# A linear-attention and max-out kernel on one core: another order of all its operations and loads

## The chip, the cores and the metric

The kernel runs on one core of a Trainium2 chip. The metric is device time in microseconds (us), taken as the median of several executions. An execution with the hardware profiler on gives a trace; its times are the span from the first instruction to the last on that core. The engines are TensorE (PE, its weight loads PEld), VectorE (DVE), ScalarE (ACT), GpSimd (POOL) and SyncE (SP), which here issues every DMA.

## The reference, cut to what matters

The first half is a recurrent attention with a decay per channel, the second a feed-forward layer whose activation is the larger of two projections. Batch 4, 8 heads, 768 tokens, head size 48; model width 384, inner width 1024.

```python
for t in range(S):
    cur = einsum('bhd,bhe->bhde', u[None] * k[:, :, t], v[:, :, t])
    y[:, :, t] = einsum('bhd,bhde->bhe', r[:, :, t], state + cur)
    state = w[:, :, t][..., None] * state + einsum('bhd,bhe->bhde', k[:, :, t], v[:, :, t])
x = y.transpose(0, 2, 1, 3).reshape(B * S, H * D)
out = maximum(x @ w1, x @ w2) @ w_out
```

## The kernel before

**Tiling.** The tokens are cut into chunks of 256, two neighbouring tokens on each of 128 partitions. There are 8 units of work: units 0 to 3 are the first chunk of batch 0, 1, 2 and 3; units 4 and 5 are the second chunk of two batches each; units 6 and 7 are the third. A chunk needs the state that the chunk before it leaves.

**A unit's steps, in the names that the order uses** (a number behind a name is the unit, further ones are a batch or a part, and @d, @a, @p mean DVE, ACT, POOL). `load` brings w, k, r, v. `wp`, `ln` and, for later units, `hi` and `lo` make logarithms of the decays; `ex` (L395 and L396, for early units L398) sums them along the tokens on PE; `mz`, `e0` (L436) and `ie` (L460) turn the sums into scale factors; `row` (L472), `wl` and `we` carry the chunk's whole decay to another layout through two small DMAs. `rk`, `ru`, `dg`, `dd`, `di` make the diagonal of the score matrix. `rw`, `kw` and `scale` give scaled r and k; `tr` and `te` transpose them on PE and copy them out (units 0 to 4), `dt` (L582) transposes by DMA (units 5 to 7). `sc` (L641) makes the scores, `mk` (L650) copies them under a mask into M, `ya` (L688) multiplies by v, `yi` (L675) adds what the old state gives, `kv` (L596) makes the new state's addend, `st`, `sm`, `sb` update the state. `vb` casts v. `xe` copies the result out of PSUM.

**The second half.** max(a, b) is relu(a − b) + b, so `wdiff` makes w1 − w2, and w2 · w_out is made once: `w2turn` and `w2take` transpose w2, `woload.0` to `woload.3` (L290) load w_out in four quarters, `wocast` casts each quarter to bf16, `wfold` (L318) multiplies, `wctake` copies out. The first matmul of every `wfold` reads the quarter of `woload.0`. Then `gt` (L706) and `rl` (L717, L719) make the relu part, `op` (L725 and L729) adds the two products, `oe` copies out and `os` (L743) stores. `hot` (L234) are 48 matmuls whose results nobody reads; they stand where PE would wait early on.

**What sets the order.** One table, ORDER, lists all 652 steps. They are recorded in this sequence, and each engine gets its instructions in it and runs them strictly one after the other. SP issues the DMAs in the table's order as well. It holds at most eight of them in flight: DMA number n waits for the landing of number n − 8, since eight semaphores take turns. Buffers are few (two tiles each for w, k, r and v, four PSUM banks for `gt`, `op`, `ex`, `wfold`, `tr` and `w2turn` together), so that a step may also wait for a buffer's last reader. The names with a number below, such as lv_174, are tiles: lw, lk, lr, lv hold loads, wso the quarters of w_out, wo_sb the cast w_out, G and Y are PSUM.

Of the kernel before, what the change touches and what calls it, by code (L numbers as in the profile page):

```python
# [59 lines left out]
rw.1.0@d wt.1.0 wload.1.2 ln.2.0 ex.2.0 vb.0.0@a we.0.1 scale.0.0.0.0@d zero.k.0@d kv.0  # L60
scale.0.0.0.1@d tr.0.0.1 dd.0@p mz.2.0 woload.0 we.1.0 ru.1.0@p kw.1.0@p row.2 w2turn.0.0 e0.1.0
scale.1.0.0.0@d st.0.0@a tr.0.0.0 te.0.0.1@a sc.0.0.1.1 sc.0.0.0.1 w2turn.0.1 dg.1 te.0.0.0@a
w2take.0.0@a wload.0.2 load.2.v scale.1.1.0.0@d dd.1@p sb.0.0@a wp.3.0@p tr.1.0.1 e0.2.0 st.0.1
te.1.0.1@a rk.2.0@d zero.M.2@p di.0.0@d ie.2.0 zero.M.0@p rw.2.0@d hot.8.1 wload.1.1 ru.2.0@d
kw.2.0@p scale.2.1.0.0@p sc.0.0.1.0 sc.0.0.0.0 mk.0.0.1.0 vb.1.0@a hot.8.4 mk.0.0.0.0 mk.0.0.1.1
mk.0.0.0.1 vb.1.1@a kv.1 scale.2.0.0.0@d tr.1.0.0 ln.3.0 te.1.0.0@a w2turn.2.1 wdiff.2@p sb.0.1@a
st.1.0@a sb.1.0@a di.1.0@d st.1.1 tr.2.0.0 w2take.0.1@a tr.2.0.1 te.2.0.1@a zero.v.0@d sc.1.0.1.0
w2turn.1.0 wload.0.0 wdiff.0@p w2take.1.0@a sc.1.0.0.0 mk.1.0.1.0 mk.1.0.0.0 sb.1.1@a w2take.2.1@d
w2turn.2.0 w2turn.1.1 w2take.2.0@a hi.3@a ya.0.0.1.0 vb.2.1@a ya.1.0.0.0 sm.0@p sm.1@p wload.0.1
wdiff.1@d ya.1.0.1.0 ya.0.0.0.1 load.3.r trih@a yi.1.0 yi.0.0 ya.0.0.0.0 woload.1 ya.0.0.1.1  # L70
xe.1.0@a xe.0.0@d load.3.k te.2.0.0@a gt.1.3 rl.1.3@a dg.2 rk.3.0@d lo.3@d dd.2@a gt.0.2 rl.0.2@a
wocast.1@p gt.1.1 w2take.1.1@d woload.3 gt.0.0 rw.3.0@p woload.2 rl.0.0@a gt.1.2 load.4.w.0 rl.1.2@a
vb.2.0@p ru.3.0@p gt.0.3 rl.0.3@a ex.3.0 wocast.3@d wocast.2@a wocast.0@a rl.1.1@a di.2.0@d
sc.2.0.1.0 mk.2.0.1.0 gt.0.1 mz.3.0 e0.3.0 kw.3.0@p gt.1.0 dg.3 sc.2.0.0.0 kv.2 st.2.0@a rl.0.1@a
wp.4.0@d ie.3.0 scale.3.0.0.0@d mk.2.0.0.0 wfold.2 sb.2.1@d wfold.0 dd.3@p ln.4.0 load.3.v st.2.1
wfold.1 sb.2.0@d vb.3.0@a wl.2 hi.4@a lo.4@d ya.2.0.0.0 load.4.r rl.1.0@a di.3.0@d vb.3.1@a row.3
ya.2.0.1.0 wctake.1@a we.2 load.4.k wctake.2@a rk.4.0@d wctake.0@a scale.3.1.0.0@p tr.3.0.0 ex.4.0
mz.4.0 tr.3.0.1 ex.4.1 mz.4.1 te.3.0.0@a kv.3 te.3.0.1@a st.3.0@a yi.2.0 xe.2.0@d ie.4.0 op.1.1
oe.1.1@a st.3.1 load.4.v e0.4.0 sb.3.0@a ru.4.0@d gt.2.0 load.5.w.0 rl.2.0@a sc.3.0.0.0 sc.3.0.1.0
vb.4.1@a gt.2.2 op.1.0 rk.4.1@p rw.4.0@d kw.4.0@d scale.4.0.0.0@d scale.4.1.1.0@d scale.4.1.0.0@p  # L80
e0.4.1 rl.2.2@a scale.4.0.1.0@d op.0.1 sb.3.1@a row.4 oe.1.0@a tr.4.1.0 te.4.1.0@a tr.4.1.1 vb.4.0@a
op.0.0 sm.2@p wl.3 mk.3.0.0.0 ya.3.0.0.0 mk.3.0.1.0 ya.3.0.1.0 yi.3.0 oe.0.1@d ru.4.1@p wp.5.0@p
we.3 sm.3@p te.4.1.1@a gt.2.1 xe.3.0@a dg.4 ln.5.0 oe.0.0@d tr.4.0.1 te.4.0.1@a gt.3.0 rl.3.0@a
rl.2.1@a hi.5@a dd.4@d load.5.k kv.4 di.4.0@d sc.4.1.1.0 load.5.r load.5.v rk.5.0@d gt.2.3 rl.2.3@a
gt.3.2 tr.4.0.0 di.4.1@d te.4.0.0@a mk.4.1.1.0 gt.3.3 st.4.0 st.4.1 os.1.0 rl.3.3@a gt.3.1 rl.3.1@a
ru.5.0@p sc.4.1.0.0 rk.5.1@p sc.4.0.0.0 load.6.r sb.4.0@a vb.5.1@a op.2.1 load.6.w.0 lo.5@d wl.4
ex.5.0 mk.4.0.0.0 os.0.0 sb.4.1@a mk.4.1.0.0 oe.2.1@a mz.5.0 e0.5.0 rw.5.0@p ex.5.1 sc.4.0.1.0
load.6.k ru.5.1@p mz.5.1 ya.4.0.0.0 scale.5.0.0.0@d op.2.0 rl.3.2@a op.3.0 mk.4.0.1.0 e0.5.1 os.1.1
scale.5.0.1.0@d dt.5.0.0 ya.4.0.1.0 dt.5.0.1 kw.5.0@d row.5 oe.3.0@d os.3.0 wp.6.0@p ie.5.0
ya.4.1.1.0 ya.4.1.0.0 oe.2.0@d yi.4.1 xe.4.1@d dg.5 dd.5@d scale.5.1.0.0@p di.5.0@d yi.4.0 xe.4.0@a  # L90
op.3.1 rk.6.0@d ln.6.0 hi.6@d gt.4.2 rl.4.2@a lo.6@d gt.4.5 scale.5.1.1.0@p rl.4.5@a os.2.1 gt.4.0
vb.5.0@a gt.4.7 rl.4.7@a we.4 sm.4@p gt.4.4 dt.5.1.0 gt.4.6 sc.5.0.1.0 mk.5.0.1.0 kv.5 oe.3.1@a
rl.4.6@a rl.4.0@a rl.4.4@a st.5.0 gt.4.1 rl.4.1@a sc.5.0.0.0 mk.5.0.0.0 gt.4.3 rl.4.3@a dt.5.1.1
rk.6.1@p st.5.1 ex.6.0 ru.6.1@p sb.5.1@a sb.5.0@a load.6.v os.0.1 vb.6.1@a mz.6.0 ex.6.1 op.4.3
load.7.w.0 load.7.k mz.6.1 e0.6.1 ie.6.0 kw.6.0@d e0.6.0 scale.6.1.1.0@p di.5.1@d sc.5.1.0.0
ya.5.0.1.0 rw.6.0@d ya.5.0.0.0 yi.5.0 xe.5.0@a vb.6.0@a scale.6.0.0.0@d op.4.2 wl.5 os.3.1
scale.6.1.0.0@p sc.5.1.1.0 oe.4.2@a op.4.0 oe.4.3@a oe.4.0@a mk.5.1.0.0 wp.7.0@p ya.5.1.0.0
mk.5.1.1.0 dt.6.0.0 ya.5.1.1.0 yi.5.1 kv.6 scale.6.0.1.0@d dt.6.0.1 xe.5.1@d st.6.0 dt.6.1.1 ln.7.0
op.4.1 sb.6.1@a sb.6.0@a oe.4.1@a ru.6.0@d dg.6 load.7.r dd.6@p gt.5.2 rl.5.2@a gt.5.4 di.6.1@d
gt.5.6 rl.5.6@a hi.7@a gt.5.0 dt.6.1.0 rl.5.0@a gt.5.3 di.6.0@d sc.6.1.1.0 rl.5.3@d rl.5.4@a  # L100
sc.6.1.0.0 gt.5.5 rl.5.5@a os.4.1 gt.5.7 rl.5.7@a rk.7.0@p lo.7@d gt.5.1 we.5 mk.6.1.1.0 rl.5.1@a
ex.7.0 op.5.1 op.5.2 oe.5.2@a sc.6.0.0.0 mk.6.1.0.0 ru.7.0@d mz.7.0 sc.6.0.1.0 mk.6.0.1.0 rk.7.1@p
ex.7.1 mk.6.0.0.0 e0.7.0 mz.7.1 op.5.3 oe.5.1@a load.7.v vb.7.1@a sm.5@p rw.7.0@p ie.7.0 os.2.0
ya.6.0.1.0 os.5.2 os.4.0 ya.6.1.0.0 ya.6.0.0.0 oe.5.3@a os.4.3 kw.7.0@p scale.7.1.1.0@p
scale.7.0.0.0@d ya.6.1.1.0 yi.6.0 xe.6.0@a scale.7.1.0.0@d dt.7.0.0 dt.7.1.0 yi.6.1 op.5.0 vb.7.0@p
xe.6.1@a gt.6.5 oe.5.0@d os.5.0 e0.7.1 gt.6.3 rl.6.3@a rl.6.5@a scale.7.0.1.0@d dt.7.1.1 gt.6.2
dt.7.0.1 os.4.2 kv.7 gt.6.6 gt.6.0 rl.6.6@a os.5.1 st.7.0 gt.6.1 rl.6.2@a ru.7.1@p dg.7 sb.7.1@a
# [690 lines left out]
```

## Time and profile before

| | |
|---|---|
| median of 3 runs | 146.53 us (146.47 to 146.93) |
| the profiled execution, span | 147.2 us |
| its instructions | 5536, of them 2403 matmuls |
| first and last matmul | start at 1.79 us, end at 143.8 us |
| DMA | 31.84 MB, mean 216 GB/s |

The profiled execution is 0.7 us longer than the median of the runs. A row of the timeline gives the start, how long the group took, the engine and line, what was written from what, the count, and in square brackets the engine's idle time ahead of it with what ended it. Matmuls overlap in their pipeline, so that a group's time has a tail that the next group runs in: the step from one start to the next is what PE pays. A row of the windows gives, for a stretch of time, each engine's busy time and count, the granted TensorE clock, the share of the DMA engines' time in use and their rate.

### The profile page before, as it was taken

Reading aid. Unit: us, or ns where it says so; the run is one execution under the profiler, and the core shown is the slowest. Engines: PE = TensorE matmul, PEld = TensorE weight load, DVE = VectorE, ACT = ScalarE, POOL = GpSimd, SP = SyncE. Lnnn points to the kernel's source line nnn. Section 1 sums busy time; section 2 is a strip of 40 time slices with the busy share of each in tenths; the row PEclk is TensorE's granted clock in tenths of the full one; section 3 lists DMA queues with packets and bytes.
Section 4 is the critical chain, followed back from the end, with each engine's and each line's share of the span. In section 5 each row is a group of like instructions: output and inputs, shape, how many; then the busy total and the mean of one; then the engine's idle time right before and its main releaser. Section 6 shows DMA issues by size and latency. Waiting matters only on the chain.

```text
span 147.2 us, 5536 instructions
## 1 busy us (share of the span) xinstructions
PE 136.8 (93%) x2403; PEld 84.2 (57%) x2404; DVE 116.9 (79%) x162; ACT 90.6 (62%) x164; POOL 90.0 (61%) x106
## 2 busy tenths in 40 slices
...
GB/s 104 323 325 357 335 401 394 366 286 304 214 241 277 212 226 282 312 255 174 205 192 177 292 251 207 141 138 291 250 136 78 131 271 20 0 210 62 4 56 157
DMA packets 71186, 31.84 MB, mean 216 GB/s; under 512 B 66293, under 2 KB 70390, under 8 KB 71162
## 3 DMA queue, kind: packets, MB, share of 16 engines
...
q8 instruction: 19, 0.31, 0.8%
q14 instruction: 5, 0.04, 0.2%
...
## 4 chain that ended last, share of the span: by engine, by line
PE 41%; DVE 35%; issue 6%; POOL 6%; DMA 4%; ACT 3%; SPq 2%; DVEq 0%; POOLq 0%; ACTq 0%
PE G L729 12%; DVE M L650 9%; PE G L706 8%; PE G L234 7%; PE G L725 5%; DVE rp L176 4%; DMA lv<-in_v_dram 4%; DVE rku L176 3%; DVE dg L502 3%; POOL kp L180 3%; DVE M L516 3%; PE Y L688 2%; SPq L582 2%; POOL rku L180 2%; PE Y L675 2%
## 5 line engine op out<-in xcount | busy, mean ns | idle before, releaser
L729 PE MATMUL G<-wo_sb,gT 128*128 128x384 bf16 x192 | 35.8, 331 | 0.0
L706 PE MATMUL G<-xT,wd_sb 128*128 128x256 bf16 (+1 forms) x192 | 34.4, 326 | 0.7 <-ACT xT L168 0.6
L650 DVE CAST_PREDICATED M<-mask,Y 128x1024 bf16<-128x1024 int32 (+1 forms) x26 | 28.6, 1131 | 2.8 <-PE Y L641 1.9
L717 ACT ACTIVATE gT<-G 128x512 bf16<-128x512 f32 x43 | 24.5, 601 | 9.8 <-PE G L706 9.6
L729 PEld LDWEIGHTS <-gT 128*128 128x128 bf16 x192 | 19.0, 99 | 12.6 <-issue 0.3
L706 PEld LDWEIGHTS <-wd_sb 128*128 128x128 bf16 x192 | 17.9, 98 | 12.6 <-DVE wd_sb L176 0.6
L180 POOL TENSOR_TENSOR kp<-lk,iE 128x384 bf16<-128x384 f32 x16 | 17.1, 1096 | 9.3 <-DVE lk L176 4.2
L725 PE MATMUL G<-wc_sb,xT 128*128 128x384 bf16 x72 | 15.7, 327 | 0.0
L180 POOL TENSOR_TENSOR rku<-rku,u_b 128x384 f32<-128x384 f32 x14 | 14.5, 1053 | 2.0 <-DVE rku L176 2.0
L234 PE MATMUL G<-S_b 128*128 128x512 bf16 x47 | 13.6, 442 | 1.8 <-DVE S_b L263 1.8
L168 ACT COPY RK<-G 128x1024 bf16<-128x1024 bf16 x12 | 12.1, 1019 | 4.7 <-PE G L565 4.7
L168 ACT COPY osb<-G 128x384 f32<-128x384 f32 x7 | 3.4, 479 | 15.9 <-PE G L729 12.6
L180 POOL TENSOR_TENSOR rku<-lr,lk 128x384 f32<-128x384 f32 x8 | 10.9, 1393 | 2.5 <-DMA lk<-in_k_dram 1.7
L641 PE MATMUL Y<-RK 48*64 48x128 bf16 x384 | 9.0, 220 | 2.6 <-DVE M L650 2.4
L502 DVE TENSOR_REDUCE dg<-rku 128x16 f32<-128x768 f32 x12 | 11.0, 945 | 0.1
L641 PEld LDWEIGHTS <-RK 48*64 48x64 bf16 x384 | 6.2, 106 | 7.8 <-issue 6.7
L168 ACT CAST xT<-Y 128x768 bf16<-128x768 f32 x7 | 7.0, 1025 | 5.3 <-PE Y L675 4.0
L168 ACT CAST S_b<-S_f 64x768 bf16<-64x768 f32 (+1 forms) x14 | 8.7, 624 | 2.3 <-DVE S_f L612 2.0
L176 DVE TENSOR_TENSOR rp<-lr,G 128x768 bf16<-128x768 f32 (+2 forms) x11 | 8.8, 799 | 1.4 <-ACT G L436 1.4
L234 PEld LDWEIGHTS <-S_b 128*128 128x128 bf16 x48 | 5.1, 112 | 8.3 <-issue 3.3
L516 DVE TENSOR_TENSOR M<-identq,gd 128x512 int32<-128x512 int32 x12 | 9.2, 778 | 0.4 <-POOL gd L168 0.3
L168 DVE CAST xT<-Y 128x768 bf16<-128x768 f32 x5 | 5.1, 1017 | 5.5 <-PE Y L688 3.2
...
## 6 DMA issues: line engine op xcount, KB each, us to landing
...
```

Of the source, the lines that this page charges most:

```text
L168: (nc.scalar.copy if e == "a" else nc.vector.tensor_copy if e == "d" else nc.gpsimd.tensor_copy)(o, i)
L176: op(o, a, b)
L180: op(o[:, g], a[:, g], b[:, g])
L234: nc.tensor.matmul(t, zz[:, 0:P], zz[:, 0:512], start=True, stop=True)
L502: nc.vector.reduce_sum(s.dg[:, b].rearrange("p i h -> p h i"), s.rku[:, b], axis=AX.X)
L516: (nc.vector if en == "d" else nc.gpsimd).tensor_tensor(out=o, in0=m, in1=g.unsqueeze(3).to_broadcast([P, 2, H, Q // 2]), op=ALU.bitwise_and)
L641: nc.tensor.matmul(t[q * Q:(q + 1) * Q, e, p * P:(p + 1) * P].rearrange("s (i g) -> s i g", i=2), s.kT[d, b, j, y * n + p, q, :], s.rT[d, ...
L650: nc.vector.copy_predicated(t[:, :, 2 * n * y:2 * n * (y + 1)].rearrange("s i (p e) g -> s p e i g", e=2), mask[:, j].bitcast(I32).unsquee ...
L706: nc.tensor.matmul(t[:, m * n * P:(m + 1) * n * P].rearrange("c (b t) -> c b t", t=P), wd_sb[:, ko, fo * P:(fo + 1) * P], s.xT[:, 0:n, ko, :],
L717: nc.scalar.activation(o, i, AF.Relu)
L725: nc.tensor.matmul(t[:, 0:HD], s.xT[:, a, ko, :], wc_sb[:, ko, :], start=(ko == 0), stop=False)
L729: nc.tensor.matmul(t[:, 0:HD], s.gT[:, c:c + P], wo_sb[:, f, :], start=False, stop=(f == FO - 1))
```

## The change

Only the table ORDER is different. It has the same 652 steps and the same 48 filler matmuls; nothing in the code of a step changes. All steps may stand at another place, and 94 of them run on another engine than before. The list was sought with a model that also counts how fast TensorE's instructions can be supplied. Four lines of the diff:

```diff
-ident zero.s.1@p identq@a load.0.k load.0.r zero.m@p identb@p u zero.s.0@d zero.r@d rk.0.0@d
...
+zero.v.0@p zero.k.1@d zero.M.0@p zero.o@p zero.k.0@d zero.s.0@d hot.8.1 hot.8.4 tri zero.M.1@d
...
+wdiff.1@p load.3.v woload.0 load.4.r wp.4.0@p wocast.0@p wfold.1 wctake.1@a dd.2@a load.4.k wfold.2
+kv.2 st.2.0@a sb.2.1@a wctake.2@a rw.3.0@d st.2.1 wl.2 kw.3.0@d ya.1.0.0.0 di.2.0@d ya.1.0.1.0
...
```

Of the 94 steps, the groups with the most work are: `scale` (6 from POOL to DVE, 1 the other way), `oe` (8 from DVE to ACT, 1 the other way), `xe` (5 from DVE to ACT, 3 the other way), `ru` (4 from POOL to DVE, 2 the other way), `wdiff` (2 from POOL to DVE, 1 the other way) and `vb` (3 from POOL to ACT).

**SP, the loads of the weights and of unit 3.** Before, from the last load of w1 on: r of unit 3, the quarter `woload.1` (wso_291, whose other half `woload.0` stands earlier), k of unit 3, the quarters 3 and 2 (wso_762), w of unit 4, v of unit 3.

```order
L285 DMA gT_383<-in_moe_w1_dram 128x1024
L372 DMA lr_220<-in_r_dram 128x8x96
L290 DMA wso_291<-in_moe_w_out_dram 128x2x384
L372 DMA lk_224<-in_k_dram 128x8x96
L290 DMA wso_762<-in_moe_w_out_dram 128x2x384 x2
L372 DMA lw_781<-in_w_dram 128x8x96 x2
L372 DMA lv_346<-in_v_dram 128x8x96
L478 DMA WL_932<-row_297 128x4x1
```

Now, from the quarters 2 and 3 (wso_336) on; the last row but one is `woload.0` (wso_214), and row_659 is `row.3`, which reads what `mz.3` wrote to MZ.

```order
L290 DMA wso_336<-in_moe_w_out_dram 128x2x384 x2
L285 DMA gT_199<-in_moe_w1_dram 128x1024
L372 DMA lr_203<-in_r_dram 128x8x96
L372 DMA lk_205<-in_k_dram 128x8x96
L285 DMA gT_257<-in_moe_w1_dram 128x1024
L472 DMA row_659<-MZ_83 1x512
L372 DMA lw_662<-in_w_dram 128x8x96 x2
L372 DMA lv_174<-in_v_dram 128x8x96
L290 DMA wso_214<-in_moe_w_out_dram 128x2x384
L372 DMA lr_672<-in_r_dram 128x8x96 x2
```

The quarter `woload.0` has moved from place 17 among the loads to place 31, behind everything that before loads up to and with v of unit 3.

**PE, the first `wfold`.** Before, it comes behind `gt` of units 0 and 1 (L706), `sc.2` (L641) and `kv.2` (L596).

```order
L706 MATMUL G_832<-xT_725,wd_sb_86 128x256
L641 LDWEIGHTS RK_497
L641 MATMUL Y_840<-RK_497 64x128
...
L596 LDWEIGHTS kp1_75
L596 MATMUL Y_857<-vp1_77,kp1_75 64x48
...
L318 LDWEIGHTS wb_548
L318 MATMUL G_897<-wo_sb_87,wb_548 128x384
```

Now it comes straight behind `sc.1.0.0.0` and `ex.3.0`.

```order
L641 MATMUL Y_635<-RK_230 64x128
L395 LDWEIGHTS wst_626
L395 MATMUL G_652<-wst_626 128x384
L396 LDWEIGHTS wst_626
L396 MATMUL G_652<-wst_626 128x384
L318 LDWEIGHTS wb_365
L318 MATMUL G_679<-wo_sb_87,wb_365 128x384
```

Fourteen steps of PE that stood ahead of the first `wfold` now stand behind it: `ya.1.0.0.0`, `ya.1.0.1.0`, `yi.1.0`, the eight `gt` of units 0 and 1, the two `sc.2`, and `kv.2`. None has come the other way.

**ACT, unit 6.** Before, the cast of one half of v (`vb.6.1`, vp1_77 from lv_2032) stands ahead of the two `e0.6` (L436).

```order
L168 CAST S_b_85<-S_f_84 64x2x8x48 x2
L168 CAST vp1_77<-lv_2032 128x8x2x48
L436 ACTIVATE G_2038<-G_2038 128x384
L460 ACTIVATE iE_2061<-MZ_83 128x768
L436 ACTIVATE G_2025<-G_2025 128x384
```

Now the two `e0.6` come first, then an `oe` (wb_2131), then the first cast of that v.

```order
L436 ACTIVATE G_2029<-G_2029 128x384
L436 ACTIVATE G_2023<-G_2023 128x384
L168 COPY wb_2131<-G_2033 128x384
L168 CAST vp1_77<-lv_1965 128x8x2x48
L168 COPY wb_2155<-G_2083 128x384
```

The scale factors of unit 6 no longer stand behind a cast that needs the load of v.

More of the change, by code (lines that the diff above doesn't have):

```diff
@@ L60 @@
[L60 to L107, printed above, removed]
@@ L113 @@
-os.7.0 op.7.2 oe.7.2@a os.7.2 oe.7.1@d os.7.1 op.7.3 oe.7.3@d os.7.3
+zero.v.0@p zero.k.1@d zero.M.0@p zero.o@p zero.k.0@d zero.s.0@d hot.8.1 hot.8.4 tri zero.M.1@d
+load.0.r mask load.0.w.0 zero.M.2@d ident zero.s.1@d load.0.w.1 wp.0.0@d ln.0.0 zero.r@d zero.m@p
+wp.0.1@d rw.0.0@d ln.0.1 rw.0.1@d ex.0.1 ex.0.0 identb@p load.0.k load.1.w.0 kw.0.0@p u rk.0.0@d
+load.1.k mz.0.1 load.2.w.0 e0.0.1 ie.0.1 uspread load.1.r wt.0.1 load.2.v mz.0.0 e0.0.0 hot.8.5
+load.0.v wt.0.0 utake@a ie.0.0 scale.0.0.0.1@d load.1.v scale.0.1.0.0@d kw.0.1@p wload.1.1 we.0.1
@@ new lines @@
+load.2.r load.2.k load.3.w.0 wload.1.2 identq@a wp.1.0@p kw.1.0@d woload.1 ln.1.0 scale.0.1.0.1@d
+tr.0.0.1 we.0.0 ru.0.0@d te.0.0.1@a ex.1.0 dg.0 hot.8.3 dd.0@a wp.2.0@p ln.2.0 rk.1.0@d ex.2.0
+ru.1.0@p mz.1.0 ie.1.0 wload.1.0 scale.0.0.0.0@d tr.0.0.0 di.0.0@d wt.1.0 mz.2.0 vb.0.1@a sc.0.0.0.1
+vb.0.0@a kv.0 wload.0.2 hot.8.0 vb.2.1@a row.2 st.0.0@a vb.1.0@a sb.0.0@a woload.2 we.1.0 e0.1.0
+st.0.1 sc.0.0.1.1 w2turn.1.0 mk.0.0.0.1 te.0.0.0@a dg.1 dd.1@a woload.3 ie.2.0 rw.1.0@p
+scale.1.0.0.0@d w2take.1.0@a vb.1.1@a e0.2.0 wload.0.1 sc.0.0.1.0 scale.1.1.0.0@p sm.0@p tr.1.0.1
```

57 lines of the change are left out of this document (47 added, 10 removed).

## The prediction
> **What bounds the kernel now.** I read the page's first part, then the windows, then PE's timeline.
>
> ```profile
> span 147.2 us, 5536 instructions
> PE 136.8 (93%) x2403; PEld 84.2 (57%) x2404; DVE 116.9 (79%) x162; ACT 90.6 (62%) x164; POOL 90.0 (61%) x106
> ```
>
> ```profile
> core 0: us, PE busy (x) PEld busy (x) DVE busy (x) ACT busy (x) POOL busy (x), PEclk, DMA share, GB/s
> 0.00:36.80 36.80, 32.46 (x458) 20.16 (x460) 31.41 (x55) 22.84 (x48) 30.61 (x49) 1.00 1.03 320
> 40.02:147.20 107.18, 101.16 (x1872) 61.69 (x1864) 82.39 (x104) 64.78 (x112) 56.20 (x55) 0.98 0.75 181
> 40.02:126.48 86.46, 83.81 (x1612) 51.74 (x1605) 76.67 (x95) 60.13 (x104) 56.20 (x55) 0.98 0.87 204
> ```
>
> PE has work nearly all the time: of the last 107.18 us it is without a matmul for 6.0, and 3.4 of these are the tail behind the last matmul at 143.8. So PE's work in this order, plus its holes, is the time. The second thing to see is the DMA share of 1.03 up to 36.8 us: the queue is full, and a load lands when all bytes ahead of it have moved. DVE is busy too, but idles 9.8 us between 40.02 and 126.48, where the last masked copy ends.
>
> PE's timeline around the first `wfold`:
>
> ```profile
> 30.79 0.91 PE L688 MATMUL Y<-M,vp 64*32 64x128 bf16 x80 [0.15 <-DVE M L650]
> 31.63 0.52 PE L675 MATMUL Y<-RK,S_b 128*32 128x128 bf16 x24
> 32.08 0.43 PE L688 MATMUL Y<-M,vp 64*32 64x128 bf16 x32
> 33.11 4.28 PE L706 MATMUL G<-xT,wd_sb 128*128 128x256 bf16 x36 [0.60 <-ACT xT L168]
> 37.22 0.33 PE L395 MATMUL G<-wst 128*128 128x384 f16 x1
> 37.39 0.33 PE L396 MATMUL G<-wst 128*128 128x384 f16 x1
> 37.64 0.42 PE L641 MATMUL Y<-RK 48*64 48x128 bf16 x16
> 37.99 1.49 PE L706 MATMUL G<-xT,wd_sb 128*128 128x256 bf16 x12
> 39.41 0.42 PE L641 MATMUL Y<-RK 48*64 48x128 bf16 x16
> 39.65 0.42 PE L596 MATMUL Y<-vp,kp 64*64 64x48 bf16 x32
> 40.02 4.06 PE L318 MATMUL G<-wo_sb,wb 128*128 128x384 bf16 x24
> ```
>
> Here `wfold` (L318) starts at 40.02 without a wait, behind `gt` (L706), two `sc` and `kv.2`. From 40.02 to the end are 107.2 us.
>
> **The change part by part.**
>
> *The hold.* The quarter `woload.0` now stands behind v of unit 3. The loads up to and with it are the very loads that before stand up to and with v of unit 3 (and one 2 KB row more). So the row of that load says when `woload.0` lands:
>
> ```profile
> 25.86 4.21 SPq L290 DMA_DIRECT2D wso<-in_moe_w_out_dram x2
> 30.17 1.32 SPq L372 DMA_DIRECT2D lw<-in_w_dram x2
> 31.53 2.77 SPq L372 DMA_DIRECT2D lv<-in_v_dram x1
> ```
>
> ```profile
> DMA to landing us min/median/max: 7.0/7.0/7.0
> ```
>
> ```profile
> 33.45 0.82 POOL L168 CAST wo_sb<-wso 128x768 bf16<-128x768 f32 x1
> ```
>
> The second is what the queries on tile lv gives for the issue at 31.53: landed at 38.5. The third is a `wocast` on POOL, 0.82. `wocast.0` is on POOL now, behind `wp.4`, which needs w of unit 4, loaded before v of unit 3. So the first `wfold.1` matmul can start at 38.5 + 0.8 = **39.4**, and hardly earlier, since the share of 1.03 leaves no DMA engine free (38.5, if all in front moves 0.9 us sooner, is my lower end).
>
> When is PE there? All that is ahead of `wfold.1` on PE now was done before by 37.64, together with `ya.1`, `yi.1` (0.9, below) and 36 matmuls of `gt` (33.11 to 37.22, 4.1). Without these PE is there at about 32.6, and waits about 6.8 us. Whatever the new start does (other first loads, memsets ahead of the first filler, DVE with more to do there), up to 6.8 us of it end in this wait and cost nothing; if that cover were gone, each us of delay would cost one.
>
> Who waits: PE is in order, so all behind `wfold.1`. On ACT `wctake.1` waits, with `dd.2` and the state of unit 2 behind it. On DVE `st.2.1` waits for `kv.2`, with `kw.3`, `di.2`, both `scale.3` and `mk.2` behind it. SP is held too: `row.3` waits for `mz.3`, hence for `ex.3` on PE at about 33.3, and w of unit 4, v of unit 3 and `woload.0` stand behind it. If the queue is empty by then, it is 8.3 us from the issue of w to the landing of v as before (30.17 to 38.5), and one load more, 0.39 MB at 320 GB/s, 1.2: start of `wfold.1` at 43.6, the upper end. Before the wait six big loads are still in flight, so I take the near row, 39.4.
>
> *What is left behind it.* PE now has these steps after the hold that it had done before 40.02, by their steps from start to start: `ya.1`, 64 of 80 in 0.84: 0.7; `yi.1`, half of 0.45: 0.2; `gt` 4.1 and 1.4; `sc.2` 0.35 and 0.24; `kv.2` 0.37. Sum **7.4**. PE's order is one queue, so nothing hides them: with no hole left they end the program 7.4 later.
>
> *The clock.* After a hole PE works slower. The hole before is at 88.7, the first matmuls after the start are the other place:
>
> ```profile
> 85.66 0.75 PE L688 MATMUL Y<-M,vp 64*32 64x128 bf16 x64
> 86.33 0.53 PE L675 MATMUL Y<-RK,S_b 128*32 128x128 bf16 x24
> 87.29 1.46 PE L729 MATMUL G<-wo_sb,gT 128*128 128x384 bf16 x8
> 90.70 0.42 PE L641 MATMUL Y<-RK 48*64 48x128 bf16 x16 [1.94 <-DVE M L650]
> 91.54 2.16 PE L729 MATMUL G<-wo_sb,gT 128*128 128x384 bf16 x8
> 93.64 1.06 PE L688 MATMUL Y<-M,vp 64*32 64x128 bf16 x64
> 94.63 0.84 PE L675 MATMUL Y<-RK,S_b 128*32 128x128 bf16 x24
> ```
>
> ```profile
> 1.79 6.10 PE L234 MATMUL G<-S_b 128*128 128x512 bf16 x16 [1.79 <-DVE S_b L263]
> 12.93 1.89 PE L234 MATMUL G<-S_b 128*128 128x512 bf16 x8
> ```
>
> After the hole of 1.94 the same three groups take 0.70, 0.31 and 0.31 longer: 1.3. At the start 16 matmuls take 6.10 where two groups of 8 would take 3.6 to 3.8: about 2.4. The new hold is longer than the first of these holes and PE runs `wfold` straight after it; I take the middle, **1.9** (0 to 2.5). The Trainium skill (TensorE: Matmul & The Clock Gate, Part 1) says that an idle window of about 3.4 us halves the clock and a busy window of about that length brings it back; by that the term would be an estimate of 1.7, and the hole of 1.94 would have cost nothing, which the rows above contradict.
>
> *What goes.* The hole at 88.7 came from the cast of v of unit 6 on ACT, which waited for its load ahead of `e0.6`:
>
> ```profile
> 86.17 0.83 ACT L168 CAST vp<-lv 128x768 bf16<-128x768 f32 x1 [0.90 <-DMA lv<-in_v_dram]
> 86.91 0.47 ACT L436 ACTIVATE G<-G 128x384 f32<-128x384 f32 x1
> ```
>
> Now `e0.6` stands ahead of that cast. I take the whole hole as gone: 1.9 + 1.3 = **3.3** less (0 to 3.9, all that PE's 6.0 us of idle leave when the tail of 3.4 is taken off, and the slow stretch). Next late there is DVE, below.
>
> *The 94 steps on other engines.* Per step, by these rows:
>
> ```profile
> L176 DVE TENSOR_TENSOR kp<-lk,iE 128x768 bf16<-128x768 f32 x2 | 2.2, 1108 | 0.1
> L180 POOL TENSOR_TENSOR kp<-lk,iE 128x384 bf16<-128x384 f32 x16 | 17.1, 1096 | 9.3 <-DVE lk L176 4.2 <-ACT iE L460 3.9 <-issue 1.1
> L176 DVE TENSOR_TENSOR rku<-rku,u_b 128x768 f32<-128x768 f32 x5 | 5.3, 1061 | 0.0
> L168 DVE COPY osb<-G 128x384 f32<-128x384 f32 x7 | 3.7, 546 | 2.5 <-PE G L729 2.5
> L168 DVE CAST xT<-Y 128x768 bf16<-128x768 f32 x5 | 5.1, 1017 | 5.5 <-PE Y L688 3.2
> ```
>
> DVE gets four full `scale` (4 x 1.1) and two `ru` net (2 x 1.1), loses two `xe` net (2 x 1.0) and seven `oe` net (7 x 0.55): +0.8; the small ones I bound by 0 to 5 more. POOL is relieved by 2 x 1.1 per full `scale`. ACT has 42 us free after 40.02. None of this is on PE's path while PE has work; I cost it at nothing, with DVE as a rival.
>
> *The sum*, in the profiled execution's time: 39.4 + 107.2 + 7.4 + 1.9 − 3.3 = 152.6. It has a span of 147.2 where the median of the runs is 146.53, so I take off 0.7: **151.9**.
>
> **The rivals.**
>
> *A, faster: the hold is short.* If `woload.0` landed when PE arrives, the sum would be 32.6 + 107.2 + 7.4 − 3.3 = 143.9, 143.2 as a median. It decides from a start of `wfold.1` at 35.9 (147.2 − 107.2 − 7.4 + 3.3, no slow clock). For it: the new order has the smaller loads first and may start its queue better. Against: the same bytes, and a share of 1.03 all the way. The chance is 0.12, of which 0.04 within 0.3%.
>
> *B, slower still: DVE becomes the bound.* After `kv.2` (39.4 + 2.7 for two thirds of `wfold` + 0.4 + 1.9 = 44.4) DVE has the 76.7 us of before, 0.8 to 5.8 more, and 20.7 from the last masked copy to the end: 142.6 to 147.6 with no idle. With the 9.8 us idle of before 152.4 to 157.4; the middle, 154.9, is 154.2 as a median. It decides from 7.5 us of idle at the middle. For it: DVE waited for PE and ACT all the time. Against: DVE loses `oe` and `xe`, both waits for PE. Chance 0.22.
>
> *C, slower, but less: nothing but the hold.* No slow clock and every other hole gone: 39.4 + 107.2 + 7.4 − 3.9 = 150.1, and 38.5 instead of 39.4 makes 149.2; as medians 149.4 and 148.5. Chance 0.16.
>
> *D: a supply of instructions is what PE lacked, and the new order spreads it.* In the trace 64 of the small matmuls L688 take 0.75 us and 80 take 0.91, 11 to 12 ns each, so a longer run is not slower; there is nothing to gain, at most the 2.6 us of holes outside the tail, which the sum counts already. Were the hold covered as well, it would be A. Chance 0.02. The Trainium skill (Runtime: NRT & Kernel Launch, Instruction fetch mechanics) also says that fetching is mostly hidden; the even 11 to 12 ns agree.
>
> **How the numbers follow.** The hold as summed has the rest, 0.48. Slower by over 0.3%, about what a measurement can tell from no change: 0.48 + 0.22 + 0.16 = 0.86. Faster: 0.08 of A and 0.01 of D, 0.09; the same: 0.05. The range goes from 148.0, a little under C, to 156.5, over B and about where the upper end of the hold leads (43.6 instead of 39.4, 156.8 with nothing else changed, hence 156.1). It leaves out A, D and little more.
>
> **What would show it.** Right: a PE row of L318 with several us idle ahead of it, released by POOL wo_sb, starting at 39 to 41; half clock behind it; `gt` of unit 0 and 1 after 43; no idle of 2 us near unit 6. Wrong: L318 starting before 36 or without idle; or the time lost in DVE's masked copies late in the program; or an L318 at 39 and an end below 149, which would mean that PE had more than 3.9 us of slack that I did not see.

## The result, and the profile after

| | before | after |
|---|---|---|
| median | 146.50 us of 4 runs (146.33 to 146.93) | 168.85 us of 4 runs (167.17 to 169.58) |
| ratio | | 1.150, 95% interval 1.1439 to 1.156 |
| profiled execution, span | 147.2 us | 165.4 us |

The change makes the kernel 15% slower, 22 us where 5 were forecast. In the experiments below some executions were in a slower state at a lower granted clock: medians and ranges are over all executions, ratios over the others alone. The page after:

```profile
span 165.4 us, 5522 instructions
PE 139.3 (84%) x2401; PEld 85.0 (51%) x2404; DVE 130.3 (79%) x165; ACT 95.5 (58%) x177; POOL 73.1 (44%) x83
DMA  5999999907999802998003999828999499004223
```

PE's work is nearly what it was, but VectorE is busy 13.4 us longer. Of the DMA engines the ninth slice (33.1 to 37.2 us) is empty, where before they were full. The windows, cut at the first `wfold`, at the end of `kv.2` and at the last masked copy's end:

```profile
core 0: us, PE busy (x) PEld busy (x) DVE busy (x) ACT busy (x) POOL busy (x), PEclk, DMA share, GB/s
0.00:45.16 45.16, 28.98 (x349) 16.83 (x353) 35.68 (x57) 23.29 (x48) 27.74 (x44) 0.92 0.90 275
45.16:165.40 120.24, 110.28 (x2052) 68.21 (x2051) 94.63 (x108) 72.20 (x129) 45.37 (x39) 0.97 0.67 162
49.83:145.75 95.92, 89.23 (x1751) 56.49 (x1749) 90.98 (x103) 65.57 (x116) 45.37 (x39) 0.98 0.73 167
```

Two losses can be read here. `wfold` starts 5.8 us later than the 39.4 of the sum, and behind it come 120.2 us, where the sum had 107.2 + 7.4 + 1.9 − 3.3 = 113.2: 7.0 more. In the last row VectorE is without work for 4.9 of 95.9 us, where it idled 9.8 of 86.5 before, and PE for 6.7. Which of the two sets the pace there the experiments test.

PE at the hold, and the three queues that make it (SP, POOL, VectorE):

```profile
33.62 0.52 PE L641 MATMUL Y<-RK 48*64 48x128 bf16 x16
35.77 0.34 PE L395 MATMUL G<-wst 128*128 128x384 f16 x1 [1.63 <-DVE wst L202]
35.94 0.33 PE L396 MATMUL G<-wst 128*128 128x384 f16 x1
45.16 4.30 PE L318 MATMUL G<-wo_sb,wb 128*128 128x384 bf16 x16 [8.89 <-POOL wo_sb L168]
```

```profile
25.80 3.98 SPq L285 DMA_DIRECT2D gT<-in_moe_w_dram  x1
36.89 0.25 SPq L472 DMA_DIRECT2D row<-MZ  x1
37.24 1.00 SPq L372 DMA_DIRECT2D lw<-in_w_dram  x2
38.29 1.25 SPq L372 DMA_DIRECT2D lv<-in_v_dram  x1
39.58 1.15 SPq L290 DMA_DIRECT2D wso<-in_moe_w_out_dram  x1
```

```profile
40.91 2.61 POOL L180 TENSOR_TENSOR lg<-lw 128x384 f32<-128x384 f32 x2 [6.74 <-DMA lw<-in_w_dram]
44.29 0.82 POOL L168 CAST wo_sb<-wso 128x768 bf16<-128x768 f32 x1 [0.77 <-DMA wso<-in_moe_w_out_dram]
```

```profile
30.88 2.16 DVE L176 TENSOR_TENSOR wd_sb<-wst 128x1024 bf16<-128x1024 f32 x1
32.96 1.75 DVE L516 TENSOR_TENSOR M<-identq,gd 128x512 int32<-128x512 int32 x1
36.31 0.56 DVE L440 TENSOR_TENSOR MZ<-G,lg 128x384 f32<-128x384 f32 x1
50.25 0.36 DVE L615 TENSOR_TENSOR T<-Y,S_f 128x192 f32<-128x192 f32 x1 [7.58 <-ACT S_f L168]
```

SP issues nothing between 29.8 and 36.9, since `row.3` stands in its queue and waits for `mz.3` (L440, 36.31), which waits for `ex.3` on PE (35.77), which waits for VectorE, where `wdiff.2` and `di.1` stand ahead of `hi.3`. Only then are w of unit 4, v of unit 3 and `woload.0` issued. PE waits 8.9 us and runs 16 matmuls of `wfold` in 4.3 us at a granted clock of 0.63 (45.16 to 49.40), and VectorE runs dry for 7.6 us.

And the hole that the sum took as gone, at unit 6:

```profile
105.72 0.42 PE L641 MATMUL Y<-RK 48*64 48x128 bf16 x16 [1.51 <-DVE M L650]
106.85 0.42 PE L641 MATMUL Y<-RK 48*64 48x128 bf16 x16 [0.71 <-DVE M L650]
```

It is still there, 2.2 us in two pieces. PE waits for VectorE's masked copies, which now have a full queue ahead of them.

### The profile page after: what moved, and what is told of

Its sections match the earlier page's. It is cut to its first block, busy times and chain, and to the rows that moved or that the text cites. A ratio compares the mean times of both kernels' runs of the same rounds, so it can differ in the third digit from the quotient of the medians.

```text
span 165.4 us, 5522 instructions
## 1 busy us (share of the span) xinstructions
PE 139.3 (84%) x2401; PEld 85.0 (51%) x2404; DVE 130.3 (79%) x165; ACT 95.5 (58%) x177; POOL 73.1 (44%) x83
## 4 chain that ended last, share of the span: by engine, by line
PE 48%; DVE 32%; issue 7%; ACT 5%; DMA 3%; POOL 2%; SPq 1%; DVEq 0%; ACTq 0%
PE G L706 12%; PE G L729 10%; PE G L234 6%; DVE rku L176 5%; PE G L725 4%; DVE kp L176 4%; PE G L318 3%; DVE M L650 3%; DMA wso<-in_moe_w_out_dram 3%; DVE dg L502 3%; PE Y L688 3%; PE Y L641 2%; DVE rp L176 2%; DVE M L516 2%; DVE lk L176 2%
## 5 line engine op out<-in xcount | busy, mean ns | idle before, releaser
L729 PE MATMUL G<-wo_sb,gT 128*128 128x384 bf16 x192 | 35.1, 326 | 0.0
L706 PE MATMUL G<-xT,wd_sb 128*128 128x256 bf16 (+1 forms) x192 | 34.0, 328 | 0.8 <-DVE xT L168 0.8
L706 PEld LDWEIGHTS <-wd_sb 128*128 128x128 bf16 x192 | 18.1, 98 | 12.7 <-DVE xT L168 1.2
L318 PE MATMUL G<-wo_sb,wb 128*128 128x384 bf16 x24 | 5.8, 406 | 8.9 <-POOL wo_sb L168 8.9
L436 ACT ACTIVATE G<-G 128x384 f32<-128x384 f32 (+1 forms) x13 | 5.8, 453 | 12.1 <-DVE MZ L440 12.0
L168 ACT CAST xT<-Y 128x768 bf16<-128x768 f32 x9 | 9.1, 1029 | 5.7 <-PE Y L675 3.6
L180 POOL TENSOR_TENSOR kp<-lk,iE 128x384 bf16<-128x384 f32 x8 | 9.7, 1228 | 5.5 <-issue 5.5
L641 PE MATMUL Y<-RK 48*64 48x128 bf16 x384 | 9.4, 220 | 2.9 <-DVE M L650 2.9
L516 DVE TENSOR_TENSOR M<-identq,gd 128x512 int32<-128x512 int32 x12 | 11.1, 938 | 0.4 <-ACT gd L168 0.4
L502 DVE TENSOR_REDUCE dg<-rku 128x16 f32<-128x768 f32 x12 | 11.0, 947 | 0.1
L688 PE MATMUL Y<-M,vp 64*32 64x128 bf16 x768 | 9.6, 226 | 1.7 <-DVE M L650 0.9
L168 ACT CAST vp<-lv 128x384 bf16<-128x384 f32 (+1 forms) x16 | 10.5, 670 | 0.0
L168 ACT COPY osb<-G 128x384 f32<-128x384 f32 x12 | 5.8, 484 | 7.4 <-PE G L729 5.6
L641 PEld LDWEIGHTS <-RK 48*64 48x64 bf16 x384 | 6.4, 106 | 7.0 <-issue 5.4
```

The source lines that it names most:

```text
L168: (nc.scalar.copy if e == "a" else nc.vector.tensor_copy if e == "d" else nc.gpsimd.tensor_copy)(o, i)
L180: op(o[:, g], a[:, g], b[:, g])
L502: nc.vector.reduce_sum(s.dg[:, b].rearrange("p i h -> p h i"), s.rku[:, b], axis=AX.X)
L641: nc.tensor.matmul(t[q * Q:(q + 1) * Q, e, p * P:(p + 1) * P].rearrange("s (i g) -> s i g", i=2), s.kT[d, b, j, y * n + p, q, :], s.rT[d, ...
L688: nc.tensor.matmul(lhsT=s.vp[g, b, 2 * p + e, j, m * 32:(m + 1) * 32], rhs=s.M[b, j][g, :, 2 * p + e, :], **into(s, b, q, p * 96 + (e + m) ...
L706: nc.tensor.matmul(t[:, m * n * P:(m + 1) * n * P].rearrange("c (b t) -> c b t", t=P), wd_sb[:, ko, fo * P:(fo + 1) * P], s.xT[:, 0:n, ko, :],
```

## The experiments

The theory after the result was that the hold makes the loss and everything behind it follows PE (hold theory). The rival was that VectorE's queue sets the pace from 60 us on (VectorE theory). Every kernel changes ORDER alone. Times are medians with their range, the kernel before ran beside each of them, and its medians lay between 146.45 and 146.79 us.

**The hold, and the two halves of the change**

One load of the new order earlier, or one small DMA later:

```diff
 e1_wo_early:      woload.1 + woload.0 ...     - load.3.v woload.0
 e2_row_late:      - mk.1.0.0.0 row.3 ...      + woload.0 row.3
```

> The changed order with one load moved: woload.0 is issued right behind woload.1, long ahead of row.3. The hold theory (the late quarter of w_out is what costs): wfold.1 then starts when PE gets there, about 36.3 instead of 45.2, with no wait for POOL wo_sb and hardly a slow clock: 168.9 - 8.9 - 2 = about 158. The DVE theory (the 94 moved steps fill VectorE, which is 98% busy from 60 to 140 us): only the 7.6 us for which VectorE stood idle at the hold come back, 161 or more, with VectorE still full to 130.

Measured: 167.88 us (166.9 to 168.32), ratio 1.1462 (1.1418 to 1.1505). Neither theory was tested, since the hold didn't go. PE's and POOL's rows:

```profile
44.20 4.34 PE L318 MATMUL G<-wo_sb,wb 128*128 128x384 bf16 x16 [8.07 <-POOL wo_sb L168]
```

```profile
40.68 2.70 POOL L180 TENSOR_TENSOR lg<-lw 128x384 f32<-128x384 f32 x2 [5.66 <-DMA lw<-in_w_dram]
43.33 0.82 POOL L168 CAST wo_sb<-wso 128x768 bf16<-128x768 f32 x1
```

The data is there, but its cast stands on POOL behind `wp.4`, whose load stands on SP behind `row.3`. The late load was one link of two.

> The changed order with row.3 moved behind woload.0, so that SP doesn't stand at row.3 until mz.3 is done (36.9 us); woload.0 keeps its late place among the loads. The hold theory, as in the prediction: the load lands at about 38.5, wfold.1 starts at about 39.4 instead of 45.2, and the time falls by 5.8 to about 163. If the queue's bytes and not SP's wait set the landing, nothing changes: 169. The DVE theory also gives 163 or a little more, so this run tells only what SP's wait is worth.

Measured: 166.23 us (165.87 to 166.93), ratio 1.1364 (1.1326 to 1.1402). The first `wfold` starts at 41.2 in place of 45.2, and only 2.6 us come off, between the two expectations. POOL's row:

```profile
39.80 1.39 POOL L168 CAST wo_sb<-wso 128x768 bf16<-128x768 f32 x1 [1.48 <-DMA wso<-in_moe_w_out_dram]
```

Without SP's wait the quarter lands at 39.8, 1.3 us later than the 38.5 of the prediction, and its cast takes 1.39 us in place of 0.82.

The change has two halves, the order and the engine choices. Each was run without the other:

```diff
 e3_engines_back:   order of after, engines (@d, @a, @p) of before
 e7_engines_only:   order of before, engines of after
```

> The changed order, all 94 moved steps back on the engines that they have before. The hold theory: the hold stays, 166 to 170. The DVE theory: VectorE's busy time falls by up to 13 us (130 to 117), of which the part behind the hold comes back: 158 to 161.

Measured: 198.52 us (195.8 to 202.6), ratio 1.3502. Both expectations were far too low.

> The order of before, with the 94 steps on the engines of the changed kernel. The hold theory: VectorE has 9.8 us of idle behind 40 us to take the 5 us more, so 146.5 to 149. The DVE theory: VectorE is nearly full from 20 to 80 us there as well and gets up to 13 us more: 152 to 158.

Measured: 170.04 us (169.2 to 170.65), ratio 1.1609 (1.1558 to 1.166). Both too low again. The 94 steps that the prediction costed at nothing cost 23.6 us in the order that was written for other engines. In the changed order the same 94 steps save 29.7 us (198.52 to 168.85). So neither half has a price of its own.

**Without the hold**

All three links taken away, then the late `ex.3` too:

```diff
 e8_hold_gone:    woload.1 + woload.0   load.3.v + row.3   + wocast.0@p ahead of wdiff.1@p
 e9_and_ex3:      as e8, and            - di.1.0@d hi.3@d lo.3@d trih@d  + hi.3@d lo.3@d trih@d di.1.0@d
```

> The changed kernel with three steps at other places, so that no part of the chain that held the first wfold is left: the quarter woload.0 right behind woload.1, row.3 behind the load of v of unit 3, and wocast.0 ahead of wdiff.1 on POOL. Both theories expect the first wfold right behind ex.3, at 36 to 37 us in place of 45.2, with no idle time of PE ahead of it and the full clock. Hold theory (the rest of the kernel follows PE): the 8.7 us and the 1.9 us of the slow clock come back, 157 to 159 us. VectorE theory (from 60 us on VectorE's queue sets the pace): only the time that VectorE stands idle around the hold comes back, 9.8 us between 40 and 60 us now against 0.1 in the kernel before, of which some 2 to 3 will stay: 161 to 162 us, and VectorE stays over 97% busy from 60 us on to 130. If the time stays over 164, something behind the hold that neither theory names sets the end.

Measured: 159.63 us (158.84 to 160.29), ratio 1.0893 (1.0837 to 1.0948): 9.2 us back, between the two expectations. `wfold` follows `ex.3` at 37.1, but still at a granted clock of 0.65 (36.5 to 41.0), 4.03 us for 16 matmuls, after a wait of PE of 1.8 us for `hi.3`, `lo.3` and `trih`.

> The kernel of the run above with one step more moved: di.1.0, 1.75 us on VectorE at 33.0, stands behind hi.3, lo.3 and trih in place of ahead of them, so that ex.3, for which PE waits 1.6 us, can start earlier. Hold theory: ex.3 and the first wfold some 1.6 us earlier, and the time 1.0 to 1.7 us below that of the run above. VectorE theory: VectorE has the same work and its queue sets the pace, so not more than 0.5 us.

Measured: 158.23 us (157.07 to 158.51), ratio 1.0772 (1.0722 to 1.0823): 1.4 us more, as the hold theory has it. `wfold` starts at 35.8 and its 16 matmuls take 2.76 us, at full clock (granted clock 1.00 from 35.8 to 38.5). So the hold as a whole is worth 10.6 us, and 11.7 us of loss are left. The windows of this kernel, 20 us each from 40 on:

```profile
40.00:60.00 20.00, 19.03 (x328) 13.48 (x311) 19.53 (x25) 16.90 (x32) 5.23 (x5) 1.00 0.98 244
60.00:80.00 20.00, 16.02 (x340) 11.48 (x341) 19.93 (x22) 14.39 (x24) 14.17 (x14) 1.00 0.43 111
80.00:100.00 20.00, 17.69 (x340) 9.83 (x339) 19.76 (x23) 11.96 (x23) 11.22 (x9) 0.93 0.97 212
```

From 60 to 100 us PE has 6.3 us without work and VectorE 0.3.

**Less work for VectorE**

A step of VectorE left out, with the hold and without it, and the control on the kernel before:

```diff
 e10_less_dve (after), e13_before_less (before), e14_e9_less_dve (e9):
-   ru.3.0  ru.5.0  ru.5.1  ru.6.0  ru.7.1
 e16_e14_no_di (e14), e17_before_no_di (e13), further:
-   di.3.0  di.4.0  di.4.1  di.5.0  di.5.1  di.6.0  di.6.1  di.7.0  di.7.1
```

> The changed kernel, hold and all, without five steps: ru.3.0, ru.5.0, ru.5.1, ru.6.0 and ru.7.1, the factor u on the diagonal of units 3, 5, 6 and 7, which is left out of the output. They are 0.96 us each on VectorE, 4.8 in all, every one behind the hold; PE's work and all other engines' work stay. VectorE theory: VectorE is 97 to 99% busy between 60 and 140 us, so 3.5 to 4.8 us come off: 164 to 165.5. Hold theory: VectorE isn't the bound, so 168 to 169.

Measured: 164.83 us (164.6 to 164.92), ratio 1.1247 (1.122 to 1.1274). 4.0 of the 4.8 us come off, as the VectorE theory has it.

> The control to the run above: the kernel before without the same five steps, the factor u on the diagonal of units 3, 5, 6 and 7, which is left out of the output. There four of them stand on GpSimd, some 8 us, and VectorE has 1 us less. Both theories: PE is the bound there and 93% busy, so within 1 us of 146.5. Should it fall by 3 us or more, then the chain from rku to the diagonal holds something up in the order before too, and the run above says less about VectorE.

Measured: 148.34 us (147.95 to 148.48), ratio 1.012 (1.0093 to 1.0146). It doesn't fall by 3 us, so the control holds. That leaving work out makes it 1.8 us slower lies outside the 1 us that was expected, and the cause stays open.

> The kernel without the hold and with the earlier ex.3 (158.2 us), and also without the steps ru.3.0, ru.5.0, ru.5.1, ru.6.0 and ru.7.1, the factor u on the diagonal of units 3, 5, 6 and 7, which is left out of the output: 4.8 us less on VectorE, all of it behind the place of the hold. With the hold in place the same step brought 4.0 us. VectorE theory: VectorE is still 96 to 99% busy from 20 to 100 us, so 3.5 to 4.8 us come off, 153.5 to 154.7, and the rest to 146.5 is mostly VectorE's too. Hold theory: the hold was all there was besides PE's own work, so not more than 1 us, 157 to 158.5.

Measured: 155.07 us (154.47 to 155.52), ratio 1.0567 (1.0523 to 1.061). 3.2 us come off without the hold: a little short of the VectorE theory, far from the hold theory.

> The kernel of the run with 4.8 us less on VectorE (155.1 us), and also without the nine di of units 3 to 7, the diagonal of the score matrix, which is left out of the output: 7 to 8.5 us less on VectorE again, at 0.78 to 0.94 us each. VectorE theory: most of it comes off as long as VectorE is the bound, 148.5 to 151. If PE's own order is the rest: PE has lost 3 us ahead of the first wfold and has the same work behind it, VectorE's share doesn't matter, 153.5 to 155.

Measured: 151.72 us (150.01 to 152.56), ratio 1.0301 (1.0228 to 1.0374). Another 3.4 us, between the two expectations, for 8.0 that VectorE is busy less (125.4 to 117.4); VectorE is the bound for part of it only.

> The control: the kernel before without the same fourteen steps, the five ru and the nine di of units 3 to 7, which are left out of the output. Without the five ru alone it took 148.3 us. Both theories: PE is the bound there, 145.5 to 148.5.

Measured: 145.93 us (145.49 to 146.39), ratio 0.9952 (0.9932 to 0.9973). The same fourteen steps are worth 0.7 us in the kernel before and 6.5 in the changed one without its hold. The comparison isn't even: four of the five `ru` are GpSimd's in the kernel before, so that VectorE is busy 6.1 us less there (116.9 to 110.8) and 13.1 here (130.5 to 117.4). PE's rows at unit 6 in this control, where the hole of the prediction was (the lines are one lower here):

```profile
89.91 0.42 PE L640 MATMUL Y<-RK 48*64 48x128 bf16 x16 [0.93 <-DVE M L649]
90.76 1.46 PE L728 MATMUL G<-wo_sb,gT 128*128 128x384 bf16 x8
```

The hole is 0.9 us and the `op` behind it takes 1.46 us for 8 matmuls, as it did ahead of the hole in the prediction; behind that hole it took 2.16.

**Which engine choices cost, in the old order**

```diff
 e11_pool_dve:  order of before, only the moves between VectorE and GpSimd
 e12_act:       order of before, only the moves from or to ScalarE
 e18_to_pool:   of e11 only VectorE to GpSimd:  rw.1.0 rw.2.0 rw.6.0 kw.5.0 kw.6.0 rk.5.0 wdiff.1 ... @d -> @p
 e19_to_dve:    of e11 only GpSimd to VectorE:  scale.3.1.0.0 ru.3.0 ru.5.0 rw.3.0 wp.5.0 wdiff.0 ... @p -> @d
```

> The kernel before, its order unchanged, with only those of the 94 engine choices that move a step between VectorE and GpSimd. By the durations of the rows VectorE gets 10 us more and GpSimd 22 us less. All 94 in the old order cost 23.6 us. Load theory (VectorE has become the bound): 3 to 10 us, at most the added work: 149.5 to 156.5, with VectorE over 97% busy wherever PE loses time. Queue theory (an engine choice costs what stands behind it in the queue of its new engine at that place in the order): 158 to 168, most of the 23.6, with VectorE idle in stretches where PE loses time, and GpSimd idle as it waits for VectorE.

Measured: 169.14 us (167.25 to 171.3). No ratio was taken; the mean of its two shortest executions, 167.25 and 168.41, is 21.2 us above the kernel before, about the queue theory's time. One place shows how, first VectorE's row and then POOL's:

```profile
106.85 0.95 DVE L176 TENSOR_TENSOR rp<-lr,G 128x768 bf16<-128x768 f32 x1 [6.54 <-POOL lr L180]
```

```profile
97.35 1.94 POOL L180 TENSOR_TENSOR lk<-lk,lw 128x384 f32<-128x384 f32 x2
103.90 1.97 POOL L180 TENSOR_TENSOR kp<-lk,iE 128x384 bf16<-128x384 f32 x2 [4.60 <-issue]
105.82 1.95 POOL L180 TENSOR_TENSOR lr<-lr,lw 128x384 f32<-128x384 f32 x2
```

`rw.6` (lr) has moved to POOL, where it stands behind a `scale` (kp) that starts at 103.90, right after ScalarE's `ie` ends (102.94 + 0.82); VectorE idles 6.5 us for it. That isn't the whole loss: from 20 to 100 us VectorE is busy 77.4 of 80 us, and PE 66.6, where it had 75.6 before. The run shows both theories at work, each in its stage.

> The kernel before, its order unchanged, with the other engine choices of the 94 only: those from or to ScalarE. VectorE has 5 us less work, ScalarE 5 us more of its 90. Load theory: no loss, 145.5 to 147.5, since neither is nearer to full than before. Queue theory: what stands behind the moved copies on ScalarE comes late, 149 to 158.

Measured: 153.34 us (151.79 to 154.9), ratio 1.0348 (1.0311 to 1.0385). By the ratio 5.1 us are lost although VectorE has less work and ScalarE is 62% busy: the queue theory's time, not the load theory's. Which of the moved copies cost it wasn't followed.

> The kernel before with only those of the engine choices that take a step from VectorE to GpSimd: rw of units 1, 2 and 6, kw of 0, 5 and 6, rk.5.0, ru of 4 and 7, wp of 1, 2 and 4, scale of unit 1, wdiff.1 and two fills. By the rows VectorE has 13.5 us less work and GpSimd 26.6 us more, 117 us in all. Load theory: GpSimd, not full at 147 us, costs little, 146.5 to 150. Queue theory: each of these steps takes twice as long and stands behind others on GpSimd, and PE waits for its result: 155 to 165.

Measured: 160.85 us (160.24 to 160.98), ratio 1.0949 (1.09 to 1.0998). The time is the queue theory's. POOL is busy 112.0 of 159.2 us, but 19.92 of the 20 between 20 and 40 us, and PE waits behind that for `wdiff.1`:

```profile
40.71 5.51 PE L706 MATMUL G<-xT,wd_sb 128*128 128x256 bf16 x26 [3.80 <-POOL wd_sb L180]
```

> The kernel before with only those of the engine choices that take a step from GpSimd to VectorE: six scale, ru of 3, 5 and 7, rw and kw of 3, rw of 5, rk.4.1 and rk.7.0, wp of 5 and 7, wdiff.0 and wdiff.2, kw of 1 and 2 and small ones. By the rows VectorE has 23.7 us more work, some 141 us in all, and GpSimd 48.6 us less. Load theory: VectorE becomes the bound with nearly all of its work ahead of 126 us, so most of the 23.7 us comes on top of it, 160 to 168. Queue theory: these steps get shorter and GpSimd's queue empties, so that the loss is smaller than in the run with both directions (22.5 us), 150 to 160.

Measured: 170.93 us (169.31 to 172.16), ratio 1.1613 (1.1532 to 1.1694). The load theory's direction, and more than its range: 24.3 us are lost, and VectorE is busy 20.7 us longer (116.9 to 137.6; the rows had given 23.7). Two of its windows:

```profile
20.00:40.00 20.00, 14.76 (x340) 10.44 (x341) 19.94 (x31) 13.87 (x27) 7.94 (x8) 1.00 1.05 323
60.00:80.00 20.00, 16.81 (x298) 11.58 (x296) 19.76 (x23) 14.33 (x22) 9.56 (x9) 0.92 0.97 248
```

VectorE is full and PE is not, in the order that was PE's before: from 20 to 100 us VectorE is busy 77.3 us and PE 64.6, where PE had 75.6. Finer windows of the kernel before show why:

```profile
20.00:40.00 20.00, 17.99 (x408) 12.86 (x406) 19.84 (x27) 16.23 (x32) 18.20 (x18) 1.00 1.03 323
40.00:60.00 20.00, 20.00 (x363) 13.53 (x352) 19.92 (x28) 17.02 (x33) 14.30 (x14) 1.00 1.00 252
60.00:80.00 20.00, 19.70 (x413) 12.44 (x414) 19.48 (x25) 15.02 (x26) 15.63 (x16) 1.00 0.96 218
80.00:100.00 20.00, 17.89 (x400) 10.80 (x398) 15.43 (x19) 12.58 (x21) 10.34 (x11) 0.91 0.94 205
```

Between 20 and 80 us VectorE idles 0.8 us in all. Of the 9.8 us that the prediction found, 9.2 lie behind 80.

**VectorE beside GpSimd**

```diff
 e15_e9_ru_pool:  e9 with  ru.3.0 ru.5.0 ru.5.1 ru.7.1  @d -> @p
 e20_e9_ru4_dve:  e9 with  ru.4.0 ru.4.1                @p -> @d
```

> The kernel without the hold and with the earlier ex.3 (158.2 us), with the factor u of units 3, 5 (both batches) and 7 (one batch) given back to GpSimd, where the kernel before has it: 3.8 us less on VectorE, 7.8 us more on GpSimd, which stands idle there for up to 14.8 us as it waits for VectorE. Load theory: 2 to 3.8 us come off, 154.4 to 156.2. Queue theory: the two on GpSimd take twice as long as on VectorE, each stands on the chain from rk to the diagonal, and what is behind it on GpSimd comes later: 158 to 162.

Measured: 157.18 us (155.96 to 158.88), ratio 1.0685 (1.0616 to 1.0755). 1.0 us below e9 with overlapping ranges, between the two expectations: inconclusive.

> The kernel without the hold and with the earlier ex.3 (158.2 us), with the factor u of both batches of unit 4 on VectorE in place of GpSimd. VectorE gets two operations of 0.95 us, 1.9 in all. Beside the four halves on GpSimd, 1.65 us each, three operations of VectorE took 1.64, 1.57 and 1.75 us (lk, kp, lr of unit 4) where the same take 0.95 elsewhere: 2.1 us more. Theory that only the sum of VectorE's operations counts: 1 to 1.9 us slower, 159.2 to 160.1. Theory that operations of VectorE and GpSimd on fp32 tiles slow each other: the three go back to 0.95 each, and the time stays within 0.7 us, 157.5 to 158.9.

Measured: 158.51 us (157.39 to 160.54), ratio 1.0784 (1.0742 to 1.0826), against 158.23: two operations more on VectorE cost nothing. VectorE's rows, first of e9, then of this kernel:

```profile
55.71 1.64 DVE L176 TENSOR_TENSOR lk<-lk,lw 128x768 f32<-128x768 f32 x1
57.45 1.57 DVE L176 TENSOR_TENSOR kp<-lk,iE 128x768 bf16<-128x768 f32 x1
58.94 1.75 DVE L176 TENSOR_TENSOR lr<-lr,lw 128x768 f32<-128x768 f32 x1
```

```profile
56.51 0.95 DVE L176 TENSOR_TENSOR lk<-lk,lw 128x768 f32<-128x768 f32 x1
57.56 0.96 DVE L176 TENSOR_TENSOR kp<-lk,iE 128x768 bf16<-128x768 f32 x1
58.44 1.75 DVE L176 TENSOR_TENSOR lr<-lr,lw 128x768 f32<-128x768 f32 x1
```

lk and kp are back at 0.95; lr isn't: POOL's next `scale` (57.69, 3.36 us for two halves) now runs beside it. For the operations the overlap theory holds. For the time it is not the only reading: the four halves of `ru.4`, 6.59 us on GpSimd in e9, are also gone from the way to the diagonal.

No kernel of these that does all the work beats the one before. The changed order at its best here, in e15 and e9, whose ranges overlap, is still 7 to 8% slower.

## Why the prediction was wrong

**The direction and the mechanism of the hold: right.** A row of L318 with idle time ahead of it, released by POOL wo_sb, half clock behind it, `gt` of units 0 and 1 behind that: all are there. Two of its signs failed, the start at 39 to 41 and the absence of 2 us of idle near unit 6.

**The start of the first `wfold`, 39.4: mis-sized, 45.2.** The step that failed is "Before the wait six big loads are still in flight, so I take the near row". The text named SP's wait at `row.3` and its end, 43.6, and took the other end. In e2, without that wait, `wfold` starts at 41.2: 4.0 of the 5.8 us are SP's wait, and the rest is the later landing and the longer cast. The wait was also longer than thought: the text had `ex.3` at 33.3, and it starts at 35.77, since VectorE's `wdiff.2` and `di.1`, 2.16 and 1.75 us where the same two take 1.21 and 0.68 in e1, stood ahead of `hi.3`. Even in e9, with the shortest way there, PE reaches the first `wfold` at 35.8 and not at 32.6. With SP blocked until 36.9, the DMA queue ran dry. POOL's queue, `wocast.0` behind `wp.4`, was named but not followed; e1 shows that this link keeps the hold even when `woload.0` is early. The hold was worth 10.6 us (168.85 to 158.23, in e8 and e9 together). The clock term, 1.9, is near: 4.30 us for 16 matmuls against 2.76 in e9, 1.5 longer.

**The hole at unit 6, −3.3: wrong.** After, 2.2 us are lost at that place (105.7), to VectorE in place of the cast. Besides, the size came from one execution. Its span is 147.2 and its mean granted clock 0.987, while the executions of the kernel before beside the experiments have spans of 144.1 to 145.6 and clocks of 0.996 to 1.0, so that half clock behind this hole isn't the rule. Their time is 1.7 to 1.9 us above their span, and the −0.7 is the sum of this and of the 2.4 us by which the profiled execution was longer. It doesn't carry over: after the change the median lies 3.5 us above the profiled span, which alone puts the forecast 4.2 us low. The other 12.8 us are the 5.8 ahead of the first `wfold` and the 7.0 behind it.

**The 94 steps, costed at nothing: the step that failed most.** "None of this is on PE's path while PE has work" rested on VectorE's idle time in one window of 86 us. That was a mean over two stages: full until 80 us, and idle behind that. In the order before, the steps that go to VectorE cost 24.3 us for 20.7 of busy time (e19), those that go to GpSimd 14.3 us (e18), those from and to ScalarE 5.1 (e12). Not every step has such a price: the two of e20 cost nothing. In the changed order 11.7 us of loss remain without the hold (e9).

**Rival B, VectorE becomes the bound: right as a mechanism, and beside the hold, not in its place.** In its terms `kv.2` ends at 49.8, VectorE has 91.0 us of work and 4.9 of idle, and 19.7 us follow the last masked copy. That these add up to the span of 165.4 proves nothing, since any span can be cut so. What speaks for the rival is that less work for VectorE brings 4.0, 3.2 and 3.4 us (e10, e14, e16), and in the old order nothing like it: e13 is 1.8 us slower than the kernel before, e17 0.7 faster. The steps left out also shorten the way from `rk` to the diagonal; e15 could have told this from VectorE's load and was inconclusive. The rival had 76.7 + 0.8 to 5.8 for the work, where 91.0 were measured, and a hold that ends 5 us earlier. Of the 13.4 us that VectorE is busy longer in all, 4.7 are the same operations taking longer (over the groups that both kernels have, the growth of the mean times the smaller count). Groups before and after, VectorE:

```profile
L502 DVE TENSOR_REDUCE dg<-rku 128x16 f32<-128x768 f32 x12 | 11.0, 945 | 0.1
L516 DVE TENSOR_TENSOR M<-identq,gd 128x512 int32<-128x512 int32 x12 | 9.2, 778 | 0.4 <-POOL gd L168 0.3
L176 DVE TENSOR_TENSOR rp<-lr,G 128x768 bf16<-128x768 f32 x8 | 7.6, 944 | 1.4 <-ACT G L436 1.4
```

```profile
L516 DVE TENSOR_TENSOR M<-identq,gd 128x512 int32<-128x512 int32 x12 | 11.1, 938 | 0.4 <-ACT gd L168 0.4
L502 DVE TENSOR_REDUCE dg<-rku 128x16 f32<-128x768 f32 x12 | 11.0, 947 | 0.1
L176 DVE TENSOR_TENSOR rp<-lr,G 128x768 bf16<-128x768 f32 x8 | 7.6, 947 | 0.1
```

**Rivals A, C and D.** A's point of decision was a start of `wfold.1` at 35.9. In e9 it is 35.8, and the kernel is still 11.7 us slower: without the hold VectorE is the bound for part of it, which A left out. C took every other hole as gone, and they grew: PE is without a matmul for 10.0 us behind the first `wfold`, where it was 6.0. For D nothing is to be seen: 64 of L688 take 0.75 us as before.

**What stays open.** Without the hold and fourteen steps of VectorE the changed order takes 151.7 us, and the kernel before without them 145.9. Of these 5.8 us some 3 may be PE's late arrival at the first `wfold`, an estimate: 35.8 in e9, where the old order stands at 40.0 with 7.4 us more done, 32.6. PE waits 1.4 us there for `hi.3`, `lo.3` and `trih` on VectorE, which take 3.6 us beside `wdiff.1` on GpSimd and 1.1 us in the changed kernel, where VectorE comes to them after it. The rest wasn't settled. Nor was it settled which steps make the 52 us of e3, nor why e13 became slower.
